# Two halves of P·V that meet in an accumulating transfer, norms of phi in two VectorE operations, and a list scheduler with other durations

## The chip, the cores and the metric

One Trainium2 chip, one of its cores. The metric is the device time of one launch in microseconds (us), the median of several runs. The engines are TensorE (PE; its weight loads are listed apart as PEld), VectorE (DVE), ScalarE (ACT), GpSimd (POOL) and SyncE (SP, which here only issues transfers).

## The reference

```python
# attention with a compressive memory; B, H, S, D = 4, 8, 576, 64
scores = where(causal, -1e9, q @ k.T / sqrt(D));  a = softmax(scores);  local = a @ v
q_p     = phi(q)                                  # phi(x) = x + 1 where x > 0, else exp(x)
mem_out = (q_p @ M_prev) / (q_p @ z_prev + 1e-6)
g       = sigmoid(beta)                           # one number for each head
x = g * mem_out + (1 - g) * local                 # -> 2304 tokens x 512
# two feed-forward layers, d_model 512, d_ff 2048
h = x @ w_in1;  x = (s * relu(h)**2 + b) @ w_out1
h = x @ w_in2;  out = (h * tanh(softplus(h))) @ w_out2
```

## The kernel before

The program has three stages that overlap. **Attention** runs as units, one for each batch b and head h. M_prev stands in front of v as 64 more keys, so that a unit is 5 row tiles of 128 queries (64 of them padding), in two groups: TA (tiles 0 to 2) and TB (tiles 3 and 4). **The first layer** (L801 and L874 on PE) works in blocks of tokens: blocks 0 to 4 of 256, then two big ones of 512; each block is 16 steps, one for each 128 columns of d_ff. **The second layer** (L1006 and L1072) follows.

Most matmuls are in float32r with each operand split into a high and a low part, so that a product costs two or three matmuls. Units of batch 0 are *early* ones: they use plain float32 with one matmul for each product and run in half units, all eight TA halves first, then the TB halves. The other 24 are *full* units. While the early units run, the first layer's weights are loaded and converted from float64, a piece at a time (32 pieces; DVE lines L705 to L718).

In a unit POOL takes min(q, 0) (L498), ACT its exp, DVE makes phi (L500). `norm_phi` (L492) multiplies phi by z and sums over 64 columns, one operation for each row tile; L496 and L504 make the reciprocal, and POOL writes the scaled phi in front of the scores in `Pt` (L555). On the other side scores (PE L534 early, L538 and L539 full) are masked and reduced on DVE (L543), exponentiated on ACT (L552), their sums inverted on DVE (L572, L574), and each tile is scaled by its row's factor (L569) on the engine that a letter string names: `E_NORM = 'PPPDA'` for early units, `F_NORM = 'PPDDA'` for full ones (P is POOL, D DVE, A ACT). PE transposes the tiles (L596) and multiplies by v (L624).

In a full unit that last product has v's high part in output rows 0 to 63 and its low part in rows 64 to 127 of one PSUM bank. ACT copies rows 64 to 127 to `xs` (L632), DVE adds rows 0 to 63 to it (L635), SP stores 64 rows to `x_d` in DRAM (L638). `load_x` reads a block of x back, four transfers into `xr` (`yr` for big blocks), once all its heads have stored (L818); ACT and DVE split it (L819, L820).

The order of work is made ahead of time by a list scheduler, `Plan`: every step has an engine, a duration, a priority and the steps that it waits for, and the next step of an engine is the ready one of the best priority. On the chip each engine works through its list in order and waits by semaphores, so that a POOL step that waits holds all POOL steps behind it. Between 7 and 85 us of the plan's clock PE is given products of zeros (L1242) where it would stand idle.

Of the kernel before, what the change touches and what calls it, by code (L numbers as in the profile page):

```python
# [37 lines left out]
E_TRA, E_NORM, E_XS = 'AAAADA', 'PPPDA', 'A'  # L38
# [19 lines left out]
def pool_us(n):  # L58
    return 0.2 + 0.0033 * n
# [272 lines left out]
def attention_then_two_ffn(ctx: ExitStack, tc: tile.TileContext, qk, qz, vm, beta,  # L332
# [99 lines left out]
    def unit(b, h, prio, groups=(TA, TB), place=None):  # L432
# [94 lines left out]
        def score(t):  # L527
# [31 lines left out]
        def norm(tiles):  # L559
# [15 lines left out]
            for t in tiles:  # L575
                e = on((E_NORM if early else F_NORM)[t])
                n = D + P * t
                us = act_us(n) if e == ACT else 0.05 + dve_us(n, True) if e == DVE else pool_us(n)
# [711 lines left out]
```

## Time and profile before

| | |
|---|---|
| median of 3 runs (lowest, highest) | 1025.32 us (1023.12, 1026.48) |
| the profiled execution | 1026.47 us, of which its span is 1024.7 |
| busy over the span | PE 98%, PEld 91%, DVE 82%, ACT 70%, POOL 20% |
| first layer's block 0 starts, its big blocks start | 81.5 us, 481.8 us |
| second layer's first matmul | 652.2 us |

A PE row's busy time counts overlapping matmuls once, and one of 256 columns is shown as 0.28 us though they follow each other every 0.12 us; so short gaps between matmuls don't show in it. Weight loads (PEld) are shorter and show them better.

### The profile page before, as it was taken

How to read it: one execution, taken by the hardware profiler on the slowest of the kernel's cores; microseconds unless marked ns; L12 is line 12 of the kernel's file. 1: busy time of each engine (PE TensorE's matmuls, PEld its weight loads, DVE VectorE, ACT ScalarE, POOL GpSimd, SP SyncE). 2: the span in 40 equal slices, each digit the busy share in tenths (PEclk: the TensorE clock that was granted, in tenths of full speed). 3: DMA queues.
4: the chain of work that ended last, by engine and by line, in shares of the span. 5: the costliest groups of instructions: out<-in, count | busy, mean ns of one | idle time of the engine just before them, and what ended most of it. 6: DMA issues, size and time to landing. Idle time of an engine off the chain costs nothing.

```text
span 1024.7 us, 20147 instructions
## 1 busy us (share of the span) xinstructions
PE 1000.5 (98%) x6738; PEld 927.6 (91%) x6738; DVE 840.1 (82%) x2403; ACT 713.2 (70%) x1606; POOL 203.9 (20%) x330
## 2 busy tenths in 40 slices
PE   6999998999999999999999999999999999999998
PEld 5567798999999999999888788899999999999998
DVE  6799999999999999996779976269975789667864
ACT  6788897888887788876878987456653466434552
POOL 6752123334333333320000000000000000100000
PEclk9899999999999999999999999999999999999999
DMA  9664662333422333315989885568686666766464
GB/s 259 181 188 142 174 187 91 108 98 105 130 88 90 91 103 92 102 49 179 271 274 305 299 275 170 211 213 269 220 299 222 217 219 205 255 224 221 145 221 170
DMA packets 88984, 188.63 MB, mean 184 GB/s; under 512 B 8752, under 2 KB 63024, under 8 KB 81584
## 3 DMA queue, kind: packets, MB, share of 16 engines
q1 hardware_dynamic: 81392, 135.95, 42.4%
q0 software_dynamic: 7056, 51.38, 14.8%
q8 instruction: 53, 0.87, 0.3%
q14 instruction: 51, 0.42, 0.1%
q10 hardware_dynamic: 432, 0.01, 0.0%
HBM read 144.32 MB, written 42.99 MB: 183 GB/s over the span
## 4 chain that ended last, share of the span: by engine, by line
PE 70%; DVE 9%; issue 7%; DMA 6%; ACT 5%; POOL 2%; SPq 0%; POOLq 0%; DVEq 0%; ACTq 0%
PE bank L1006 15%; PE bank L1072 14%; PE bank L874 13%; PE bank L801 13%; PE bank L624 5%; PE bank L596 4%; PE bank L534 2%; DMA wi_d<-sc 2%; PE bank L538 1%; PE bank L539 1%; POOL Pt L569 1%; DMA stage<-in_w_in 1%; DMA woh<-wo_split_d 1%; PE bank L1242 1%; DMA x_d<-xs 1%
## 5 line engine op out<-in xcount | busy, mean ns | idle before, releaser
L1072 PE MATMUL bank<-woh,S 128*128 128x256 f32 x792 | 107.4, 283 | 1.4 <-DMA woh<-wo_split_d 1.4
L1072 PEld LDWEIGHTS bank<-woh,S 128*128 128x128 f32 x792 | 100.8, 192 | 1.6 <-ACT S L729 1.6
L1072 PE MATMUL bank<-wol,S 128*128 128x256 f32 x720 | 98.1, 283 | 0.0
L555 POOL TENSOR_SCALAR Pt<-ex,nm 128x64 f32<-128x64 f32 x148 | 73.3, 513 | 105.6 <-DVE nm L504 56.3
L1006 PE MATMUL bank<-wi,woh 128*128 128x384 f32 x426 | 93.9, 334 | 0.0
L552 ACT ACTIVATE Pt<-Pt,mx 128x64 f32<-128x64 f32 (+4 forms) x148 | 81.3, 551 | 18.0 <-DVE mx L543 17.7
L1072 PEld LDWEIGHTS bank<-wol,S 128*128 128x128 f32 x720 | 91.8, 192 | 0.0
L987 POOL DMA_DIRECT2D wol<-wo_split_d x17 | 9.2, 541 | 354.1 <-DVE wi L730 262.3
L1006 PEld LDWEIGHTS bank<-wi,woh 128*128 128x128 f32 x426 | 75.6, 188 | 0.6
L1006 PE MATMUL bank<-wi,wol 128*128 128x384 f32 x294 | 75.9, 334 | 0.0
L596 PE MATMUL bank<-ident,Pt 128*128 128x128 f32 x432 | 65.1, 277 | 8.0 <-POOL Pt L569 6.3
L569 POOL TENSOR_SCALAR Pt<-Pt,rs 128x64 f32<-128x64 f32 (+2 forms) x68 | 52.4, 806 | 77.1 <-DVE rs L574 44.6
L543 DVE CUSTOM_DVE_ANT_0 Pt<-bank,mask 128x320 f32<-128x320 f32 (+3 forms) x148 | 59.5, 419 | 9.5 <-PE bank L534 5.2
L604 DVE TENSOR_TENSOR PTl<-bank,PTh 128x128 fp32r<-128x128 f32 (+1 forms) x144 | 64.5, 481 | 1.3 <-ACT PTh L601 0.8
L596 PEld LDWEIGHTS bank<-ident,Pt 128*128 128x128 f32 x432 | 48.7, 141 | 14.2 <-POOL Pt L569 10.5
L601 ACT CAST PTh<-bank 128x128 fp32r<-128x128 f32 (+1 forms) x144 | 54.4, 430 | 4.2 <-PE bank L596 2.4
L1006 PEld LDWEIGHTS bank<-wi,wol 128*128 128x128 f32 x294 | 53.1, 188 | 0.3
L874 PE MATMUL bank<-gl,woh 128*128 128x256 f32 x320 | 53.2, 289 | 0.0
L874 PE MATMUL bank<-gh,wol 128*128 128x256 f32 x320 | 53.2, 288 | 0.0
L874 PE MATMUL bank<-gh,woh 128*128 128x256 f32 x320 | 52.3, 286 | 0.0
L801 PE MATMUL bank<-xh,wi 128*128 128x256 f32 x320 | 50.1, 287 | 0.3 <-DVE rt L852 0.2
L624 PE MATMUL bank<-PTh,V 128*128 128x384 f32 (+1 forms) x192 | 48.1, 277 | 0.0
(277 smaller groups left out, 2894.4 us busy)
## 6 DMA issues: line engine op xcount, KB each, us to landing
wol<-wo_split_d POOLq DMA_DIRECT2D x17, 1024.0 KB, 5.2
woh<-wo_split_d POOLq DMA_DIRECT2D x16, 1024.0 KB, 5.5
qk<-in_qk SPq DMA_DIRECT2D x24, 608.0 KB, 3.9
stage<-in_w_out SPq DMA_DIRECT2D x23, 512.0 KB, 4.9
wo_split_d<-high SPq DMA_DIRECT2D x44, 256.0 KB, 4.3
stage<-in_w_in SPq DMA_DIRECT2D x21, 512.0 KB, 5.2
stage<-wi_d SPq DMA_DIRECT2D x24, 384.0 KB, 5.4
wi_split_d<-woh SPq DMA_DIRECT2D x8, 1024.0 KB, 4.9
```

Source lines behind the costliest of these rows:

```text
L543: nc.vector.tensor_tensor_reduce(Pt[t].t[:, D + lo:D + hi], ps.t[:, :hi - lo], mask[:, SP - w + lo:SP - w + hi], -SCALE, mx.t[:, t:t + 1] ...
L552: nc.scalar.activation(Pt[t].t[:, D:w + D], Pt[t].t[:, D:w + D], AF.Exp, bias=mx.t[:, t + i:t + i + 1], scale=-1.0, accum_out=rs.t[:, t:t ...
L555: add(POOL, 0.3, lambda: nc.gpsimd.tensor_scalar(Pt[t].t[:, :D], ex.t[:, t, :], nm.t[:, t:t + 1], 1.0, op0=ALU.mult, op1=ALU.mult), [ex, n ...
L569: (nc.vector if e == DVE else nc.gpsimd).tensor_scalar(x, x, r, None, op0=ALU.mult)
L596: nc.tensor.transpose(ps.t[:, c - c0, :], Pt[t].t[:, c * P:(c + 1) * P], ident)
L601: (nc.vector.tensor_copy if dve else nc.scalar.copy)(PT[0].t[:, at_], ps.t[:, :n])
L604: nc.vector.tensor_tensor(PT[1].t[:, at_], ps.t[:, :n], PT[0].t[:, at_].bitcast(F32), op=ALU.subtract)
L624: nc.tensor.matmul(o.rearrange("p (t q) -> p t q", q=P), v, x.t[:, f[0]:f[-1] + 1:f[1] - f[0] if len(f) > 1 else 1, :], start=(c == 0 and ...
L801: nc.tensor.matmul(ph, w_at(nm, r, cc)[:, o:o + P], x_at(x, cc), start=(part == 0 and cc == 0), stop=(part == 2 and cc == NCC - 1))
L874: nc.tensor.matmul(acc[ec // per].t[:, (ec % per) * n:(ec % per + 1) * n], w_at(nm, r, jj)[:, ec * P:(ec + 1) * P], t(x), start=(big and f ...
L1006: nc.tensor.matmul(ps.t[:, :H2], w[i // 4].t[:, j, kk, i % 4], x[kk].t[:, k], start=begin and part == kk == 0, stop=part == 2 and kk == 1, ...
L1072: nc.tensor.matmul(acc[t].t[:, :DH], s.t[:, j, t * P:(t + 1) * P], x.t[:, k, q % 4], start=q == part == 0, stop=q == NQ2 - 1 and part == 2)
```

## The change

There are three edits. First, in full units ACT copies all 128 rows of the product to `xs`, the DVE addition goes, and SP stores both halves, to two tensors `x_d[0]` and `x_d[1]`. `load_x` reads `x_d[0]` as before and then POOL issues a second transfer that adds `x_d[1]` to the same tile; it waits for the first to land. It is there for the columns of full units only: 4 of 192 columns in block 2, 4 of 256 in each of blocks 3 and 4, 4 of 512 in each big block; 20 in all, and none for blocks 0 and 1. Second, `norm_phi` becomes one product over all the tiles of a unit and one reduction. Third, the scheduler gets other durations, hops and landing times, and the third letter of `E_NORM` goes from POOL to DVE.

```diff
-E_TRA, E_NORM, E_XS = 'AAAADA', 'PPPDA', 'A'
+E_TRA, E_NORM = 'AAAADA', 'PPDDA'
+ACCUM_LAG = 4.5
 def pool_us(n):
-    return 0.2 + 0.0033 * n
+    return 0.38 + 0.0028 * n
...
         def norm_phi():
-            for t in tiles:
-                nc.vector.tensor_tensor_reduce(qn()[:, t + 1, :], ex.t[:, t, :], qn()[:, 0, :], 1.0, 0.0,
-                                               ALU.mult, ALU.add, nm.t[:, t:t + 1])
+            nc.vector.tensor_tensor(q_rows(), ex.t[:, mine], qn()[:, 0:1, :].to_broadcast([P, n_t, D]), op=ALU.mult)
+            nc.vector.tensor_reduce(nm.t[:, mine], q_rows(), axis=AXIS, op=ALU.add)
...
-            add(POOL, 0.3, lambda: nc.gpsimd.tensor_scalar(Pt[t].t[:, :D], ex.t[:, t, :], nm.t[:, t:t + 1], 1.0,
+            add(POOL, 0.48, lambda: nc.gpsimd.tensor_scalar(Pt[t].t[:, :D], ex.t[:, t, :], nm.t[:, t:t + 1], 1.0,
...
-            if not early:
-                add(DVE, dve_us(m), lambda: nc.vector.tensor_tensor(xs.t[:, :m], pv.t[:D, skip:n], xs.t[:, :m], op=ALU.add),
-                    [pv, xs], [xs])
+            rows = slice(0, D) if early else slice(0, P)
+            add(ACT, act_us(m) - 0.04, lambda: nc.scalar.copy(xs.t[rows, :m], pv.t[rows, skip:n]), [pv], [xs])
-            add(DMA, 0.5, lambda: nc.sync.dma_start(x_d[p0:p0 + D, h // 2, c0:c0 + m], xs.t[:, :m]), [xs], [x_in[b, groups_all.index(g)]])
+            for i in range(1 if early else 2):
+                add(DMA, 0.3, lambda i=i: nc.sync.dma_start(x_d[i][p0:p0 + D, h // 2, c0:c0 + m], xs.t[i * D:(i + 1) * D, :m]),
+                    [xs], [x_in[b, groups_all.index(g)]])
...
+            if n > skip:
+                add(POOL, 1.0, prio, lambda c=c, xr=xr: nc.gpsimd.dma_start(xr.t[:, skip:], x_d[1][:, c, t0 + skip:t0 + n], accum_op=ALU.add,
+                                                                            max_dma_last_dim=1024), [*need, xr], [xr]).lag = ACCUM_LAG
```

The changed program has 2104 DVE rows where there were 2382, 347 POOL rows for 335, 112 stores of x for 64, and 113 products of zeros for 144; the other matmuls are the same in number. Its line numbers are up to 3 higher (L569 becomes L572, L555 L558, L498 L501, L635 goes). Three places show how the order moves.

POOL in the first stage, from the first early TA half on (`Pt_0_158` and its like are the half's three tiles, `B_0_235` a third tile held elsewhere); before:

```order
L569 TENSOR_SCALAR Pt_0_158<-Pt_0_158,rs_160 128x64
L569 TENSOR_SCALAR Pt_0_162<-Pt_0_162,rs_160 128x192
L569 TENSOR_SCALAR Pt_0_174<-Pt_0_174,rs_160 128x320
L555 TENSOR_SCALAR Pt_1_226<-ex_182,nm_212 128x64
L555 TENSOR_SCALAR Pt_1_231<-ex_182,nm_212 128x64
L555 TENSOR_SCALAR B_0_235<-ex_182,nm_212 128x64
L498 TENSOR_SCALAR ex_278<-qn_153 128x192
```

and of the change:

```order
L572 TENSOR_SCALAR Pt_0_168<-Pt_0_168,rs_170 128x64
L572 TENSOR_SCALAR Pt_0_172<-Pt_0_172,rs_170 128x192
L558 TENSOR_SCALAR Pt_1_208<-ex_178,nm_199 128x64
L558 TENSOR_SCALAR Pt_1_214<-ex_178,nm_199 128x64
L558 TENSOR_SCALAR B_0_222<-ex_178,nm_199 128x64
L501 TENSOR_SCALAR ex_260<-qn_148 128x192
```

The half's widest scaling (320 columns) has left POOL; it now stands on DVE. This is so for all eight TA halves.

DVE in a full unit of batch 1, from the last two of its five row sums; before:

```order
L492 ISA qn_2533,nm_2692<-ex_2588,qn_2533 128x64
L492 ISA nm_2692 128x1
L492 ISA qn_2533,nm_2692<-ex_2588,qn_2533 128x64
L492 ISA nm_2692 128x1
L635 TENSOR_TENSOR xs_2707<-bank_112,xs_2707 64x256
L572 TENSOR_SCALAR rs_2650<-rs_2650,igate 128x3
```

and of the change, the like place of another such unit:

```order
L495 TENSOR_TENSOR qn_2974<-ex_3021,qn_2974 128x320
L496 TENSOR_REDUCE nm_3143<-qn_2974 128x5
L499 TENSOR_SCALAR nm_3143<-nm_3143,igate 128x5
L575 TENSOR_SCALAR rs_3091<-rs_3091,igate 128x3
```

Five pairs have become two instructions, and the addition to `xs` is gone.

POOL where block 2 of the first layer is loaded, in both programs from row 157, min(q, 0) of the tenth full unit, on; before:

```order
L498 TENSOR_SCALAR ex_3357<-qn_3297 128x320
L555 TENSOR_SCALAR Pt_0_3455<-ex_3145,nm_3276 128x64
L555 TENSOR_SCALAR Pt_0_3484<-ex_3145,nm_3276 128x64
L555 TENSOR_SCALAR Pt_0_3488<-ex_3145,nm_3276 128x64
```

and of the change:

```order
L501 TENSOR_SCALAR ex_3398<-qn_3346 128x320
L820 DMA xr_3376<-x_d 128x192
L820 DMA xr_3386<-x_d 128x192
L820 DMA xr_3391<-x_d 128x192
L820 DMA xr_3403<-x_d 128x192
L558 TENSOR_SCALAR Pt_1_3450<-ex_3206,nm_3318 128x64
L558 TENSOR_SCALAR Pt_1_3483<-ex_3206,nm_3318 128x64
```

Four accumulating transfers stand ahead of the next unit's L558, each behind a wait for its tile's first load.

Counted in the two orders, before and in the change: ahead of block 0's first L801 PE has 133 and 113 attention matmuls; ahead of its first L820 DVE has 32 and 29 row minima and 15 and 13 converted pieces. Between the TA product of the eighth full unit, the last that block 2 needs, and block 2's first matmul PE has 65 and 132 matmuls. Between attention's last matmul and the first big block's PE has 132 and 180. From the first big block on the markers of the order agree.

## Rows read from the trace of the kernel before

**Rows 1.** Stretches: length, PE, PEld, DVE, ACT, POOL busy, clock, DMA.

```profile
0.00:81.50 81.50, 69.31 (x343) 48.47 (x343) 65.24 (x254) 62.20 (x166) 51.35 (x76) 0.94 0.71 205
81.50:158.40 76.90, 76.32 (x527) 65.27 (x527) 72.97 (x232) 68.68 (x156) 17.98 (x24) 1.00 0.55 165
158.40:481.80 323.40, 317.93 (x2539) 308.41 (x2538) 296.61 (x1120) 259.00 (x684) 108.50 (x182) 1.00 0.34 101
481.80:675.00 193.20, 192.18 (x883) 161.20 (x882) 139.81 (x282) 145.86 (x271) 0.00 (x0) 1.00 0.77 249
675.00:1024.70 349.70, 344.79 (x2453) 344.24 (x2451) 265.47 (x519) 177.50 (x331) 26.08 (x49) 1.00 0.67 225
...
30.00:40.00 10.00, 8.00 (x27) 5.34 (x26) 6.36 (x24) 5.78 (x17) 6.00 (x10) 0.66 0.62 167
```

**Rows 2.** Chain that ended last, 0 to 82 us: start, length, what.

```profile
22.18 1.44 POOL B L569
...
25.84 1.08 POOL Pt L569
26.92 3.70 POOL Pt L555 x2
...
58.73 1.54 POOL Pt L569
```

**Rows 3.** POOL's groups, 0 to 81.5 us: count, busy us, mean ns, idle before.

```profile
L569 POOL TENSOR_SCALAR Pt<-Pt,rs 128x320 f32<-128x320 f32 x4 | 5.6, 1398 | 0.0
L569 POOL TENSOR_SCALAR B<-B,rs 128x320 f32<-128x320 f32 x4 | 4.8, 1212 | 0.0
```

**Rows 4.** DVE's groups over the whole span, the same columns.

```profile
L569 DVE TENSOR_SCALAR Pt<-Pt,rs 128x320 f32<-128x320 f32 x24 | 9.9, 412 | 0.0
L635 DVE TENSOR_TENSOR xs<-bank,xs 64x320 f32<-64x320 f32 x24 | 11.5, 478 | 2.6 <-ACT xs L632 2.4
L635 DVE TENSOR_TENSOR xs<-bank,xs 64x256 f32<-64x256 f32 x24 | 9.9, 414 | 3.8 <-ACT xs L632 3.5
```

**Rows 5.** DVE's timeline in a full unit, 212.7 to 214.2 us: start, length, instruction.

```profile
212.41 0.49 DVE L500 SCALAR_TENSOR_TENSOR ex<-qn,ex 128x320 f32<-128x320 f32 x1
212.82 0.48 DVE L635 TENSOR_TENSOR xs<-bank,xs 64x320 f32<-64x320 f32 x1
213.22 0.22 DVE L492 CUSTOM_DVE_ANT_0 qn<-ex,qn 128x64 f32<-128x64 f32 x1
213.37 0.07 DVE L492 DVE_READ_ACCUMULATOR2_ANT nm<- 128x1 f32 x1
...
214.02 0.47 DVE L857 SCALAR_TENSOR_TENSOR gl<-rt,sb,gh 128x256 fp32r<-128x256 f32 x1
```

**Rows 6.** Weight loads, 81.5 to 481.8 us; last, PEld's idle time by releaser.

```profile
L596 PEld LDWEIGHTS bank<-ident,Pt 128*128 128x128 f32 x387 | 43.4, 140 | 6.6 <-POOL Pt L569 3.8 <-issue 1.1 <-DVE Pt L569 0.6
L801 PEld LDWEIGHTS bank<-xh,wi 128*128 128x128 f32 x320 | 42.8, 190 | 1.7 <-DVE rt L852 0.9 <-issue 0.5
L624 PEld LDWEIGHTS bank<-PTl,V 128*128 128x128 f32 x192 | 36.5, 190 | 2.0 <-DVE PTl L604 2.0
L539 PEld LDWEIGHTS bank<-B,A 128*128 128x128 f32 x144 | 27.4, 190 | 2.1 <-DVE B L513 1.8
L538 PEld LDWEIGHTS bank<-B,A 128*128 128x128 f32 x144 | 27.3, 190 | 3.2 <-DVE PTl L604 1.5 <-DVE xs L635 0.8 <-DVE PTl L601 0.2
```

**Rows 7.** Timelines: x of block 2, its first matmuls, big x.

```profile
250.82 0.45 SPq L638 DMA_DIRECT2D x_d<-xs  x1
252.04 3.72 SPq L818 DMA_DIRECT2D xr<-x_d  x4
258.51 1.77 PE L801 MATMUL bank<-xh,wi 128*128 128x256 f32 x10
...
466.96 0.45 SPq L638 DMA_DIRECT2D x_d<-xs  x1
469.01 1.76 SPq L818 DMA_DIRECT2D yr<-x_d  x4
481.80 0.86 PE L801 MATMUL bank<-yh,wi 128*128 128x512 f32 x3
```

**Rows 8.** Issues on POOL (ns); KB and us to landing.

```profile
L987 POOL DMA_DIRECT2D wol<-wo_split_d x17: 527/528/737, 715.8 to 999.9; - x17
wol<-wo_split_d POOLq DMA_DIRECT2D x17, 1024.0 KB, 5.2
xr<-x_d SPq DMA_DIRECT2D x20, 128.0 KB, 3.5
yr<-x_d SPq DMA_DIRECT2D x8, 256.0 KB, 6.4
```

**Rows 9.** L555 on POOL: shortest, median, longest ns; DVE beside the longest (timeline).

```profile
L555 POOL TENSOR_SCALAR Pt<-ex,nm x148: 307/353/3097, 6.8 to 452.9; 128x64 f32<-128x64 f32 x148
26.05 0.86 DVE L709 CUSTOM_DVE_ANT_0 stage<-wil,stage 128x1024 uint16<-128x1024 uint16 x1
28.61 0.69 DVE L718 TENSOR_TENSOR wi<-stage,wi 128x512 fp32r<-128x512 f32 x1
```

More of the change, by code (lines that the diff above doesn't have):

```diff
@@ L375, in attention_then_two_ffn @@
     sb = const.tile([P, 2], F32, name="sb")
-    x_d = dram.tile([P, NCC, NT], F32, name="x_d")
+    x_d = [dram.tile([P, NCC, NT], F32, name=f"x{i}_d") for i in range(2)]
     y_d = dram.tile([P, NCC, NT], F32, name="y_d")
@@ L432, in unit, with add @@
     def unit(b, h, prio, groups=(TA, TB), place=None):
-        def add(engine, us, f, r=(), w=(), keep=(), share=1.0):
+        def add(engine, us, f, r=(), w=(), keep=(), share=1.0, lag=0.0):
             attention_steps.append(plan.add(engine, us, prio, f, r, w, keep=keep, share=share))
+            attention_steps[-1].lag = lag
         early = place is not None and place < 5
         first_half = groups == (TA,)
+        late = 1.3 if early else 0.0
         tiles = [t for g in groups for t in g]
@@ L577, in norm @@
                 n = D + P * t
-                us = act_us(n) if e == ACT else 0.05 + dve_us(n, True) if e == DVE else pool_us(n)
+                us = act_us(n, 1) if e == ACT else 0.08 + dve_us(n, True) if e == DVE else pool_us(n)
                 add(e, us, lambda t=t, e=e: scale(t, e), [done, Pt[t]], [Pt[t]], [rs])
@@ L642, in unit @@
         norm(groups[0])
[L643 removed]
+        add(DMA, 0.6 * nb / NQ, lambda: nc.sync.dma_start(vx(), vm[b, h][:, :nb]), w=[vx_b], lag=late)
         if not early:
@@ L691, in convert @@
         add(DMA, 1.5, prio, lambda: nc.sync.dma_start(words(), src.bitcast(I32).rearrange("p (n two) -> p n two", two=2)),
-            w=[raw], after=after).lag = 1.0 if layer == 1 else 3.0
+            w=[raw], after=after).lag = 1.4 if layer == 1 else 3.0
         e = on((C_W if layer == 1 else C2_W)[j])
-        add(e, 0.52 if e == ACT else 0.335, prio,
+        add(e, 0.567 if e == ACT else 0.335, prio,
             (lambda: nc.scalar.activation(f32(), words()[:, :, 1].bitcast(F32), AF.Copy, scale=2.0 ** -112)) if e == ACT else
@@ L845, in first @@
             add(PE, 0.48 if not big else 0.908, prio, lambda part=part: mm_in(ph.t[:, :n], xh, xl, fc, part), need, [ph])
-        add(ACT, act_us(n) - 0.04, ew, lambda: nc.scalar.activation(
+        add(ACT, act_us(n) - (0.04 if big else -0.06), ew, lambda: nc.scalar.activation(
             rt.t, ph.t[:, :n], *((AF.Relu,) if big else (AF.Copy, 0.0, sb[:, 0:1]))), [ph], [rt])
@@ L853, in first @@
                 [ph, rt], [rt])
-        add(ACT, act_us(n), ew, (lambda: nc.scalar.copy(t(gh), rt.t)) if big else
+        add(ACT, act_us(n) + (0.0 if big else 0.1), ew, (lambda: nc.scalar.copy(t(gh), rt.t)) if big else
             (lambda: nc.scalar.activation(t(gh), rt.t, AF.Identity, sb[:, 1:2])), [rt], gh_bufs + ([gg] if big else []))
-        add(DVE, dve_us(n), ew, (lambda: nc.vector.tensor_tensor(t(gl), rt.t, t(gh).bitcast(F32), op=ALU.subtract)) if big else
+        add(DVE, dve_us(n) + (0.0 if big else 0.06), ew, (lambda: nc.vector.tensor_tensor(t(gl), rt.t, t(gh).bitcast(F32), op=ALU.subtract)) if big else
             (lambda: nc.vector.scalar_tensor_tensor(t(gl), rt.t, sb[:, 1:2], t(gh).bitcast(F32), op0=ALU.add, op1=ALU.subtract)),
```

30 lines of the change are left out of this document (13 added, 17 removed).

## The prediction

> **What bounds the kernel now.** I read the stages first [rows 1]. From 81.5 us on, PE is busy 99%, 98%, 99% and 99% of the stretches, and in the last one the weight loads too (344 of 350 us). From 481.8 us on PE alone sets the time, and the order there is the same in both programs; a gain has to come from before. Before 81.5 us no engine is full: PE 69.3, DVE 65.2, ACT 62.2 and POOL 51.4 of 81.5 us, and PE's figure holds 143 products of zeros. This stage waits in a chain, for block 0 of the first layer can't begin before all eight TA halves are stored. From 81.5 to 481.8 us PE and DVE are both nearly full (DVE 73.0 of 76.9 us, then 296.6 of 323.4), so that each loses a little to the other.
>
> Second, the chain of the first stage [rows 2]: POOL carries much of it, the widest scalings of tiles among them (1.44, 1.08, 1.54 us), and a pair of L555 that took 3.70 us. Third, who ended PEld's idle time in the middle stage [rows 6]: DVE 7.8 us (0.6, 0.9, 2.0, 1.8, and 1.5 + 0.8 + 0.2), POOL's L569 3.8. These 11.6 us are all that other engines visibly take from PE in 400 us.
>
> **The first stage: -4 us.** Eight 320-column scalings leave POOL, 5.6 + 4.8 = 10.4 us [rows 3]. Three of them stand on the chain with 1.44 + 1.08 + 1.54 = 4.06 us [rows 2]. On DVE one takes 0.41 us [rows 4], 3.3 us in all, on an engine that is free 16 us of this stage. Bounds: 10.4 us if every one held a half up, nothing if DVE is as late as POOL was. I take 4, what the chain shows.
>
> The new order also puts less ahead of block 0: 13 converted pieces for 15, 29 row minima for 32. That is about a tenth of DVE's 65.2 us, 6.5, less the 3.3 that it takes over: 3 us. So block 0 starts near 74.5 us. But what was put off is done later, when PE is full: 20 attention matmuls at the next stretch's pace (527 in 76.9 us, 0.146 each) are 2.9 us. Of the 7 us 4 stay. Bounds: +1 (the chain doesn't shorten, the deferred work costs) and -8 (10.4 + 3 - 2.9, less 2.5 for the L555 that then lead).
>
> The norm in two operations costs these halves about what it cost; POOL's better known durations only reorder.
>
> **The middle stage: -4 us.** In 24 full units the additions to `xs` go. A DVE operation here holds the engine some 0.08 us less than its length: the 0.48 us one at 212.82 is followed at 213.22, after 0.40 [rows 5]. So 24 x (0.40 + 0.33) = 17.5 us leave DVE [rows 4].
>
> The norms: five row sums ran from 213.22 to 214.02, 0.80 us, the reads of the accumulator beside the next operation [rows 5]. The new pair are two passes over 320 columns. A product or a copying operation of that width holds DVE 0.40 us (L500 at 212.41, L635 at 212.82), a scaling 0.41 - 0.08 = 0.33 [rows 4, 5]; a reduction isn't in the trace. From 2 x 0.33 to 0.40 + 0.80, if the reduction needs twice the time, a unit wins 0.14 or loses 0.40, over 24 units -3 to +10 us of DVE. I take 0.80, no change, as the reduction reads the same columns once.
>
> [...] In the trace five short sums cost what I give two long operations [rows 5]. [...]
>
> What are 17.5 us of 369.6 us of DVE worth? If DVE alone set the pace, all of it; if PE did, nothing. PE's visible waits for DVE are 7.8 us [rows 6], and the two engines fill up alike. I take half of these waits, 4 us, and put the rest at what PE needs anyway. ACT copies 128 rows instead of 64 with the same columns, no more time. SP has 48 more stores of 0.45 us [rows 7], spread over the 320 us of the full units; the loads queued behind one come 0.45 us later, which the units in flight hide.
>
> **The accumulating transfers: 0.** Block 2 is the place where x is late. Before, its last store is issued at 250.82 and its first matmul starts at 258.51, 7.7 us [rows 7]. The change adds the second store (0.45), four issues on POOL (0.53 each, 2.1) and one more landing. The landing of an accumulating transfer isn't in the trace: 3.5 us for a plain load of 128 KB by SP is the nearest below, 5.2 for 1024 KB issued by POOL the nearest above [rows 8]. The chain then takes 13.8 to 15.5 us. The order has 132 matmuls between the product that feeds that store and block 2, at 2539 in 323.4 us [rows 1] 16.8 us of work; before it had 65, 8.3 us, for a chain of 7.7. So the cover has grown with the chain, by a little over a microsecond to spare. Without it PE would lose up to the landing, 5 us.
>
> Each transfer waits in POOL's queue for its tile's first load, and behind the four stand the next unit's L558; who waits for those is PE's transposes. A hold of 2 us there is inside what POOL has free (108.5 of 323.4 us busy). For the first big block, before, the last store is issued at 466.96, its loads from 469.01, and its first matmul is at 481.80 [rows 7]; the loads take 6.4 us [rows 8], so x and its split are there by about 478. With the transfers it is some 8 us later, while the order now has 180 matmuls there for 132, 5.8 us more cover besides the 4 that were free. Blocks 3 and 4 are loaded far ahead of their use. From the first big block on nothing changes.
>
> **The sum.** The profiled execution took 1026.47 us, its span 1024.7 and 1.8 around it. 1026.5 - 4 - 4 + 0 = 1018.5. It stands 1.2 above the median of the runs shown, so a median of the changed kernel should be near 1017.
>
> **Rivals.**
>
> *POOL's queue becomes the wait (slower).* An operation on POOL can be stretched by DVE: L555 takes 0.31 us at its shortest and 3.10 at its longest, and beside the longest DVE ran L709 and L718, which read two inputs from SBUF [rows 9]. If DVE does that to the accumulating issues, four take 12.4 us instead of 2.1: block 2's x is 10.3 us later, 9 beyond the cover, and at half speed without the first layer PE loses 4.5 there; the L558 behind are held as long at blocks 2, 3 and 4, about 4 us of PE each time beyond what two units in flight hide. That is 16 us, 1033. It decides from issues of about 1.5 us on. Against it: POOL's plain issues took 0.527 to 0.737 us [rows 8], beside a DVE busy for 265 of 350 us [rows 1]. [...] Chance 0.14.
>
> *The gain is taken back (no change).* If the first stage waits for DVE's conversions rather than POOL, only 3 us come, 2.9 are paid later, and if in the middle PE is bound by its own stream, the freed DVE time is idle: 1025. For it speaks that PE's busy figure is 98% there. Chance 0.20.
>
> *DVE is the real bound of the middle stage.* Then the 17.5 us come off whole, with 4 in the first stage: 1026.5 - 21.5 - 1.2 = 1004. DVE's 95% between 81.5 and 158.4 us speaks for it; but there it converts weights, which doesn't change, and later it is at 92%. Chance 0.17.
>
> [...]
>
> **How the numbers follow.** My forecast, 1017, has 0.45, with 1010 to 1022.2 as its own range. DVE as the bound has 0.17, around 1004; no change 0.20, between 1022 and 1028; POOL's queue 0.14, from 1028 up to 1040; 0.04 is for what I don't see. 0.3% of 1025.3 is 3.1 us, about what a measurement of this kernel can tell from no change. Faster: 0.45 + 0.17 + 0.04 of the third = 0.66; within 0.3%: 0.17; slower: 0.17. The range from 1005 to 1029 leaves out half of the DVE case and most of the slow one, about 0.2.
>
> **What the profile will show.** Block 0's first matmul near 74.5 us (81.5 now), the first big block's near 473.8 (481.8), and the same 543 us from there to the end. POOL's 320-column scalings gone and the first stage's POOL at about 41 us; DVE in the middle stage near 352 us for 369.6; the two operations of the norm near 0.80 us together; the accumulating issues at 0.53 us, their landings at 3.5 to 5.2; PE's wait for block 2 under 1 us. Wrong, if the landings take over 6.5 us (block 2 starves), if block 0 doesn't come earlier, or if PE's idle time for DVE vanishes and matmul counts rise to those of the last stage (then DVE was the bound).

## The result and the profile after

The changed kernel took 1031.97 us in the median of four runs (1030.65 to 1033.81), the kernel before 1025.69 beside it: a ratio of 1.0067, with an interval from 1.0043 to 1.0091. It is 0.67% slower, where 1017 us was forecast. Its profiled execution took 1030.65 us, 4.2 more than that of before.

The stretches of the changed kernel, cut at the same times as [rows 1], columns as there:

```profile
0.00:81.50 81.50, 71.01 (x371) 50.37 (x372) 70.86 (x232) 66.36 (x177) 43.81 (x68) 1.00 0.72 208
81.50:158.40 76.90, 74.20 (x505) 62.50 (x503) 72.28 (x203) 65.42 (x148) 15.60 (x24) 1.00 0.49 157
158.40:481.80 323.40, 311.55 (x2492) 307.18 (x2493) 283.38 (x894) 254.72 (x685) 126.59 (x201) 0.98 0.45 122
481.80:675.00 193.20, 191.70 (x878) 159.67 (x877) 135.25 (x278) 142.35 (x266) 1.20 (x1) 1.00 0.79 252
675.00:1028.70 353.70, 348.18 (x2468) 347.04 (x2466) 266.23 (x519) 178.95 (x333) 26.09 (x49) 1.00 0.66 222
```

DVE lost 13.2 us in the third stretch and POOL 7.5 in the first, as the change meant. But PE has 47 matmuls fewer in the third stretch and its clock a mean of 0.98: something there keeps it waiting. The first matmul of the first layer came at 68.1 us (81.5 before), yet the first big block's at 483.0 (481.8).

To find where a lead goes, I count PE's work by the widths of the matmuls that have begun (0.06 us for 128 columns up to 0.227 for 512, more for the plain float32 ones of the early halves, where 256 columns follow each other every 0.216 us and full units' every 0.120; products of zeros left out). It is 936 us in every kernel here. The table, computed from the traces, gives the time at which the kernel before has done so much, and how much later (+) or earlier (-) the others have. It is one execution of each, which can stand a few us from its median: e9 is the same program as the changed kernel up to 249 us, and yet stands 4.8 us from it at work 117. What a kernel loses from one column to the next varies less: from 80 to 117 the changed kernel, e3, e9 and e10, all the same program up to there, lose 10.1 to 10.9 us.

```
work done          20     80    110    117    190    240    385    400    480    560    930
before           55.9  130.9  163.7  175.0  253.2  308.5  464.2  479.4  559.6  641.1 1015.1
after            -6.7   -9.3   -6.0   +0.8   +0.1   -2.2   -6.5   +1.2   +1.7   +2.8   +4.0
e1 accum alone   -3.1   -3.9   -2.1   +2.7   +1.7   +3.7   +4.2   +9.6  +11.8  +15.7  +16.2
e2 no accum      -5.8   -9.2   -2.5   -1.7   -2.0   +0.4   -0.3   -0.4   -0.4   -2.1   -1.9
e3 loads behind  -5.5   -7.8   -4.6   +2.8   +2.0   +0.6   -1.7   -1.8   -1.8   -1.6   -1.6
e5 norm on POOL  -0.2   -3.2   -1.6   +0.3   +0.4   +8.2   +5.4   +6.3   +6.5   +9.8  +10.5
e6 low on POOL   -4.1   -5.7   -0.8   +5.4   +4.1   +3.5   +5.0   +5.5   +5.5   +5.8   +6.2
e7 units later   -6.8   -9.2   -5.9   +0.4   -1.3   -0.5   -3.9   -3.7   -3.7   -3.8   -3.2
e8 e2 + e6       -6.3   -9.0   -4.4   -3.0   -4.1   -5.0   -7.1   -7.2   -7.2   -8.9   -8.7
e9 plain second  -2.5   -5.3   -2.1   +5.6   +5.8   +3.8   +0.7   +4.5   +4.5   +3.5   +4.9
e10 no transfer  -6.2   -9.0   -5.6   +1.4   +0.8   -2.1   -5.6   -5.7   -5.7   -7.4   -9.0
e13 low twice    -4.0   -5.9   +0.3   +9.3   +8.6   +7.7   +5.0   +7.5  +12.6  +15.2  +15.8
e14 low to POOL  -6.2   -8.9   -5.2   +1.8   +1.2   -0.8   -4.1   +0.6   +3.0   +4.8   +3.5
e17 less DVE     -6.8   -9.2   -5.7   +0.8   +0.1   -1.5   -5.3   -1.2   -0.6   +0.9   -0.5
e18 durations    -2.4   -5.8   +0.6   +0.2   +0.4   +2.6   +1.2   +1.1   +1.1   -0.5   +0.3
```

So the change gains twice and loses twice: 9.3 us ahead at 131 us, all lost by 176 (6.8 of it after 158); 6.6 us gained between 253 and 458; 7.7 lost at once at the first big block; 2.8 more after it.

**The first loss.** Windows of 5 us of the changed kernel, same columns:

```profile
150.00:155.00 5.00, 4.96 (x42) 4.76 (x41) 5.00 (x14) 4.99 (x12) 0.00 (x0) 1.00 0.28 82
155.00:160.00 5.00, 3.56 (x28) 3.14 (x26) 4.91 (x11) 3.65 (x8) 1.99 (x2) 1.00 0.33 85
160.00:165.00 5.00, 1.97 (x11) 1.51 (x11) 4.93 (x20) 3.59 (x11) 2.41 (x5) 1.00 0.58 204
165.00:170.00 5.00, 2.69 (x11) 1.96 (x11) 4.92 (x14) 4.25 (x10) 2.06 (x3) 0.64 0.13 39
170.00:175.00 5.00, 4.93 (x30) 4.93 (x31) 4.30 (x11) 2.50 (x6) 3.25 (x6) 0.68 0.39 113
```

DVE is full while PE stands, and after PE's idling the clock is granted at 0.64 and 0.68 in the last two windows. The waits from 150 to 172 us (engine, line, releaser: total, times, longest):

```profile
POOL Pt L558 <- DVE nm L507: 8.9, 2, 8.4
PEld bank L599 <- POOL Pt L572: 3.6, 2, 3.0
PE bank L599 <- POOL Pt L572: 3.2, 2, 2.8
PEld bank L542 <- DVE B L516: 1.8, 1, 1.8
PEld bank L627 <- DVE PTl L607: 1.8, 1, 1.8
```

These belong to the first full units, which go through ACT, DVE and POOL in turn while the last weights are still converted.

**The second loss.** Windows of the changed kernel at the first big block:

```profile
460.00:465.00 5.00, 5.00 (x44) 5.00 (x44) 1.82 (x4) 1.46 (x3) 3.72 (x3) 1.00 0.82 240
465.00:470.00 5.00, 4.59 (x39) 4.39 (x37) 0.00 (x0) 0.00 (x0) 1.21 (x1) 1.00 1.04 257
470.00:475.00 5.00, 0.45 (x2) 0.45 (x3) 1.92 (x4) 2.49 (x5) 0.00 (x0) 0.86 0.96 160
475.00:480.00 5.00, 5.00 (x25) 5.00 (x25) 4.65 (x11) 4.87 (x10) 2.39 (x3) 0.50 0.67 180
```

SP's queue there, and under it POOL's (timelines: start, length, instruction):

```profile
456.88 2.74 SPq L818 DMA_DIRECT2D yr<-x_d  x4
459.67 0.91 SPq L691 DMA_DIRECT2D stage<-in_w_in  x2
460.62 0.43 SPq L691 DMA_DIRECT2D raw<-in_w_in  x1
```

```profile
460.43 3.72 POOL L820 DMA_DIRECT2D yr<-x_d  x3 [15.20 <-DMA yr<-x_d]
465.49 1.21 POOL L820 DMA_DIRECT2D yr<-x_d  x1 [1.33 <-DMA yr<-x_d]
```

The waits from 465 to 482 us, and the DMA issues from 455 to 477 us (KB each, median us to landing):

```profile
ACT yh L822 <- DMA yr<-x_d: 8.7, 2, 8.5
PEld bank L801 <- DVE rt L855: 5.2, 1, 5.2
```

```profile
yr<-x_d POOLq DMA_DIRECT2D x4, 256.0 KB, 12.1
raw<-in_w_in SPq DMA_DIRECT2D x1, 512.0 KB, 11.1
```

The first halves are issued from 456.9 us; behind them SP at once issues three loads of second-layer weights, 1.5 MB; the accumulating transfers are issued from 460.4 us, beside and behind these, and land 10.9 to 13.0 us after issue, all after the three loads. ACT stands in order at the split of x (8.5 us), so the products that the first layer still has to do get no new input (PE's wait for L855), PE is busy 0.45 of 5 us, and then it runs 5 us with the clock granted at 0.50. Before, the first big block's x came whole with the four loads issued from 469.01 us [rows 7], ahead of the weight loads.

### The profile page after: what moved, and what is told of

The parts are those of the page before. It is cut to its first block, busy times and chain, and to the rows that moved or that the text cites. A ratio compares the mean times of both kernels' runs of the same rounds, so it can differ in the third digit from the quotient of the medians.

```text
span 1028.7 us, 19852 instructions
## 1 busy us (share of the span) xinstructions
PE 996.6 (97%) x6707; PEld 926.8 (90%) x6707; DVE 828.0 (80%) x2123; ACT 707.8 (69%) x1606; POOL 213.3 (21%) x342
## 4 chain that ended last, share of the span: by engine, by line
PE 68%; issue 17%; DMA 6%; DVE 5%; POOL 2%; ACT 2%; SPq 0%; POOLq 0%; ACTq 0%; DVEq 0%
PE bank L877 18%; PE bank L801 18%; PE bank L1009 9%; PE bank L1075 6%; PE bank L627 6%; PE bank L599 5%; PE bank L542 2%; PE bank L537 2%; PE bank L541 1%; DMA yr<-x_d 1%; DMA xr<-x_d 1%; DMA woh<-wo_split_d 1%; DMA woh<-wi_split_d 1%; DMA x_d<-xs 1%; DVE Pt L546 1%
## 5 line engine op out<-in xcount | busy, mean ns | idle before, releaser
L558 POOL TENSOR_SCALAR Pt<-ex,nm 128x64 f32<-128x64 f32 x148 | 75.7, 571 | 121.7 <-PE bank L599 80.2
L555 ACT ACTIVATE Pt<-Pt,mx 128x64 f32<-128x64 f32 (+4 forms) x148 | 81.6, 553 | 9.7 <-DVE mx L546 8.9
L1009 PEld LDWEIGHTS bank<-wi,woh 128*128 128x128 f32 x450 | 79.5, 188 | 0.9 <-DMA woh<-wi_split_d 0.3
L1009 PE MATMUL bank<-wi,wol 128*128 128x384 f32 x270 | 69.5, 335 | 0.1
L546 DVE CUSTOM_DVE_ANT_0 Pt<-bank,mask 128x320 f32<-128x320 f32 (+3 forms) x148 | 60.3, 419 | 4.0 <-PE bank L537 2.1
L572 POOL TENSOR_SCALAR Pt<-Pt,rs 128x64 f32<-128x64 f32 x64 | 48.5, 830 | 53.8 <-DVE rs L577 31.3
L801 PE MATMUL bank<-xh,wi 128*128 128x256 f32 x320 | 50.8, 287 | 0.1
L1009 PEld LDWEIGHTS bank<-wi,wol 128*128 128x128 f32 x270 | 48.7, 188 | 0.6 <-DMA wol<-wi_split_d 0.3
```

The costliest lines, as they stand in the source:

```text
L546: nc.vector.tensor_tensor_reduce(Pt[t].t[:, D + lo:D + hi], ps.t[:, :hi - lo], mask[:, SP - w + lo:SP - w + hi], -SCALE, mx.t[:, t:t + 1] ...
L555: nc.scalar.activation(Pt[t].t[:, D:w + D], Pt[t].t[:, D:w + D], AF.Exp, bias=mx.t[:, t + i:t + i + 1], scale=-1.0, accum_out=rs.t[:, t:t ...
L558: add(POOL, 0.48, lambda: nc.gpsimd.tensor_scalar(Pt[t].t[:, :D], ex.t[:, t, :], nm.t[:, t:t + 1], 1.0, op0=ALU.mult, op1=ALU.mult), [ex, ...
L572: (nc.vector if e == DVE else nc.gpsimd).tensor_scalar(x, x, r, None, op0=ALU.mult)
L801: nc.tensor.matmul(ph, w_at(nm, r, cc)[:, o:o + P], x_at(x, cc), start=(part == 0 and cc == 0), stop=(part == 2 and cc == NCC - 1))
L1009: nc.tensor.matmul(ps.t[:, :H2], w[i // 4].t[:, j, kk, i % 4], x[kk].t[:, k], start=begin and part == kk == 0, stop=part == 2 and kk == 1, ...
```

## The experiments

Each ran in five rounds beside the kernel before (1024.5 to 1026.1 us there). The ratios:

| run | median us | ratio to before, interval |
|---|---|---|
| e1 accum alone | 1042.59 | 1.0162, 1.0131 to 1.0193 |
| e2 no accum | 1024.45 | 0.9983, 0.9970 to 0.9996 |
| e3 loads behind | 1025.17 | 0.9994, 0.9977 to 1.0011 |
| e4 five sums | 1035.34 | 1.0078, 1.0054 to 1.0102 |
| e5 norm on POOL | 1034.51 | 1.0098, 1.0076 to 1.0120 |
| e6 low on POOL | 1032.71 | 1.0083, 1.0064 to 1.0101 |
| e7 units later | 1024.76 | 1.0004, 0.9991 to 1.0017 |
| e8 e2 and e6 | 1018.13 | 0.9940, 0.9922 to 0.9958 |
| e9 plain second | 1026.98 | 1.0019, 0.9999 to 1.0039 |
| e10 no transfer | 1021.28 | 0.9956, 0.9939 to 0.9974 |
| e11 2 KB pieces | 1032.59 | 1.0077, 1.0048 to 1.0106 |
| e12 before, low on POOL | 1025.78 | 0.9995, 0.9980 to 1.0010 |
| e13 low twice | 1036.11 | 1.0104, 1.0077 to 1.0131 |
| e14 low to POOL, same order | 1035.02 | 1.0079, 1.0054 to 1.0105 |
| e15 scalings to DVE | 1037.38 | 1.0104, 1.0082 to 1.0126 |
| e16 accum in batch 1 | 1025.16 | 0.9995, 0.9982 to 1.0008 |
| e17 less DVE | 1030.16 | 1.0051, 1.0035 to 1.0067 |
| e18 durations alone | 1025.10 | 0.9996, 0.9984 to 1.0008 |

### The parts of the change

**e1**, the kernel before with the diff's parts on `xs`, `x_d` and `load_x` alone.

> The kernel before with the accumulating transfers alone (both halves stored, the second added on loading); norms, durations and the order's numbers stay those of before. My theory (the gain is real, and is taken back at the first big block, whose four accumulating transfers queue behind 1.5 MB of second-layer weight loads): the last PV product ends 4 to 10 us before 465.8 us, the first big block's four transfers land 9 to 13 us after their issue and it starts no earlier than 478 us; time 1021 to 1028 us. Rival one (accumulating transfers are slow whatever is beside them): also the blocks of 256 columns wait, the starts of blocks 2 to 4 move later by 3 us or more against before; time over 1030 us. Rival two (the loss comes from the new durations, not from the transfers): the first big block starts by 474 us, time 1012 to 1019 us.

The landings (10.4 to 11.1 us) and the big block's late start (491.4) came as the theory had them. The time did not, nor did the last product of P and v, which ends 1.7 us earlier than before and not 4 to 10. Rival one's signs came too: blocks 2 to 4 begin 7 to 12 us later. The old order has less cover: it loses 5.4 us at the first big block and 3.9 at the second. Rival two is out.

**e2**, the changed kernel with these parts undone.

> The changed kernel without the accumulating transfers: the two halves are added on DVE as before, with the new norms, durations and order numbers. My theory: the gap at 468 to 475 us and the half-clock stretch behind it go, DVE's 17.5 us of additions come back; the first big block starts at 470 to 477 us, the stall at 150 to 175 us stays; time 1019 to 1026 us, under the changed kernel by 5 us or more. Rival two (new durations and order lose by themselves): the stall at 150 to 175 us is as large and the time is 1029 us or more.

As the theory had it, 8.6 us under the changed kernel in ratio; no loss at the big block. Only the block's start, 481.4 us, is not at 470 to 477. PE still loses 7.5 us of lead by 175 us, so that loss isn't the transfers'. The dense stretch gains nothing here (-2.0 to -0.3), where the changed kernel gained 6.6.

**e4** and **e18**, the five sums of the norms put back into the orders of the changed kernel and of e2.

```diff
-            nc.vector.tensor_tensor(q_rows(), ex.t[:, mine], ..., op=ALU.mult)
-            nc.vector.tensor_reduce(nm.t[:, mine], q_rows(), axis=AXIS, op=ALU.add)
+            for t in tiles:
+                nc.vector.tensor_tensor_reduce(...)
```

> The changed kernel with the norms of phi as before (five multiply-and-sum operations of 64 columns in place of a product and a sum over 320), in the same order of instructions on every engine. My theory (the two forms cost the same, 0.80 us a unit): within 0.3% of the changed kernel, 1029 to 1035 us. Rival three (the two-operation form is the loss): 1024 us or less; if it is instead a gain on DVE, 1036 us or more.

> The kernel of e2 with the norms as before the change (five sums), in e2's order: the kernel before with the new durations and the moved scaling alone. If the two forms of the norms cost the same (my prediction), within 0.2% of e2, 1022 to 1027 us. If the new form saves DVE time (e4 against the changed kernel points to 1 us or so), 1025 to 1029 us.

The sums cost 0.11% and 0.13% against the pair, within the intervals. The durations and the moved scaling by themselves change nothing (0.9996).

### The first big block

**e3**, the weight loads behind the transfers.

```diff
-        add(DMA, 1.5, prio, lambda: nc.sync.dma_start(words(), ...), w=[raw], after=after)
+        behind = layer == 2 and len(raw_steps) < 3 * 6
+        queue = nc.gpsimd if behind else nc.sync
+        add(POOL if behind else DMA, ..., -2.0 if behind else prio, lambda: queue.dma_start(words(), ...),
+            w=[raw], after=[*after, *accumulated] if behind else after)
```

> The changed kernel with one thing moved: the first three second-layer weight loads (512 KB each) are issued on POOL's queue behind the first big block's four accumulating transfers, not on SP's ahead of them. My theory (queueing behind these loads): the four transfers land 4 to 7 us after issue in place of 10.9 to 13.0 us, the first big block starts at 472 to 477 us in place of 483, no half clock behind it; time 1021 to 1026 us. Rival one (accumulating 256 KB is slow by itself, 3 to 4 us each, one after another): they still land 9 to 13 us after issue, time 1029 to 1033 us.

The four landed after 4.8, 5.3, 6.5 and 7.1 us. The first big block started at 480.1, since this execution's earlier stages were later too, and no work was lost there (-1.7 to -1.8 in the table). Up to 474 us PE, DVE and ACT work in the changed kernel's order, so that nothing else stands between the two. The windows of e3:

```profile
465.00:470.00 5.00, 5.00 (x44) 5.00 (x43) 1.69 (x4) 1.68 (x4) 4.90 (x4) 1.00 0.90 198
470.00:475.00 5.00, 5.00 (x44) 5.00 (x43) 2.90 (x5) 2.60 (x6) 1.68 (x3) 1.00 1.12 197
475.00:480.00 5.00, 5.00 (x43) 4.97 (x42) 2.73 (x6) 2.88 (x7) 0.29 (x1) 1.00 0.96 319
```

PE stays full (5.00 of 5 us) and its clock at 1.00. Where the three loads stand is worth 0.73%, 7.5 us, as much as the change had lost.

**e9**, the second transfers as plain loads.

```diff
-  nc.gpsimd.dma_start(xr.t[:, skip:], x_d[1][...], accum_op=ALU.add, max_dma_last_dim=1024)
+  nc.gpsimd.dma_start(xr.t[:, skip:], x_d[1][...], max_dma_last_dim=1024)
```

> The changed kernel with its second transfers of x as plain loads, not accumulating ones: the same bytes, queue, waits and order on every engine, but the second half overwrites the first and is not added, so the output is not the reference's. It separates what accumulating costs from what one more transfer behind the first costs. If the price is the queueing behind the weight loads (my theory of the first big block), the four transfers of the first big block still land 9 to 12 us after issue and the time is 1029 to 1033 us. Rival (adding on the way into SBUF makes the transfers slow): they land within 4 to 7 us, those of block 2 within 4 us in place of 3.0 to 7.7, and the time is 1022 to 1027 us.

Both have a part. The first big block's transfers landed after 8.7 to 9.7 us, as the theory had it, so most of the delay is the queue. Adding makes them longer: 10.9 to 13.0 us in the changed kernel, 9.1 to 11.9 in the six other runs of its order (e4, e11, e13 to e15 and e17). In blocks 2 to 4 it is 2.4 to 5.5 us plain and 3.0 to 7.8 accumulating, the third and fourth of a group the slow ones. The time, 1026.98 us, is in the rival's range: leaving out the adding alone gives back 0.48%, 4.9 us. How much of that is at the big block, one execution doesn't settle: the loss there is 3.8 us for 7.7, but e14 and e17, which add, lose 4.8 and 4.1.

**e11**, `max_dma_last_dim=2048` for 1024.

> The changed kernel with rows of 2 KB in the big blocks' accumulating transfers in place of two pieces of 1 KB (the size argument 2048 for 1024); all else the same. If the pieces' number sets the landing (rival), the big blocks' transfers land 3 us or more sooner and the time is 1025 to 1029 us; if it is the queueing behind the weight loads (my theory), they land within 1 us of before and the time stays at 1030 to 1034 us.

No change, as the theory had it: landings of 10.5 to 11.7 us, a ratio of 1.0077.

**e10**, the second transfers left out (`if n > skip` made false).

> The changed kernel without the second transfers of x at all: both halves are stored, the second is never read, so the output is not the reference's; the order is planned anew. It gives what freeing DVE of the additions, the new norms and the new durations bring when nothing has to be paid for them. My prediction's steps (4 us in the first stage, 4 us in the middle, nothing lost afterwards): 1014 to 1020 us. Rival (DVE's bound at 125 to 175 us eats it all; the additions off DVE are worth nothing): within 2 us of e2, 1022 to 1026 us.

0.9956, between the two ranges and 0.27% under e2 (the intervals just overlap): freed of its price, taking the additions off DVE is worth some 3 us, and the change as a whole 4.5. Its profiled execution, 3.7 us under its median, shows the same loss at 158 to 176 us and a gain of 6.4 in the dense stretch.

**e16**, accumulating for batch 1 alone.

```diff
+LAST_ACCUM = 1
...
+            added = b > LAST_ACCUM
...
+        top = min(n, (LAST_ACCUM + 1) * S - t0)
...
-            if n > skip:
+            if top > skip:
```

> The changed kernel with the accumulating transfers for the second batch's x alone (8 units, blocks 2 to 4); the 16 units of the last two batches add their halves on DVE and store one x, so the big blocks have no second transfer; planned anew. If accumulating pays where no weight loads are queued ahead: a third of e10's dense-stage gain over e2 stays (2 us), 1019 to 1023 us. Rival (it costs in blocks 2 to 4 what it frees): as e2 or slower, 1024 to 1030 us.

The rival held: 0.9995, no better than e2.

### The stretch up to 176 us

**e7**, `UNIT0` 92.65 for 84.65, on e3.

> The kernel of e3 with the priorities of the full attention units and of the first layer's blocks 8 us later (one number of the plan), nothing else changed. My theory (DVE is the bound at 125 to 175 us, whatever comes first): the place of the stall moves, but the starts of blocks 2 and 3 stay within 2 us of e3's 261.8 and 341.2 and the time within 3 us of e3. Rival (the full units were started too early, on top of the weight conversions): the stall falls to about the 8 us of the kernel before, time 1016 to 1021 us.

The time is e3's, as the theory had it (block 3 came 3.3 us sooner), and the loss between 131 and 175 us is 9.6 us for e3's 10.6. But this is no test of the stall: the new priorities leave the orders of PE, ACT and DVE as they are in e3 up to 163 us. Neither later nor earlier units were tried there.

**e5**, e3 with `E_NORM` 'PPPDA'.

> The kernel of e3 (weight loads behind the transfers), with the scaling of the third attention tile in the early units back on POOL, as before the change (eight operations of 320 columns, 0.40 us each on DVE), and the order planned anew. My theory (between 125 and 175 us DVE is the bound, so that a unit's work moved onto DVE earlier is paid there): 3.2 us less on DVE, the stall at 125 to 175 us (17 us of PE's time in e3, 8 in the kernel before) shrinks by 2 to 4 us, though block 0 starts later than in e3, and the time is 1020 to 1024 us. Rival (the order of the units makes the stall): stall unchanged within 1.5 us, time 1024 to 1030 us.

Half right, and the time wrong. The loss between 131 and 175 us is 3.5 us for e3's 10.6, but the lead was only 3.2. Then, in this order, block 2's transfers were issued from 254.4 and the last landed at 264.7 too late for PE:

```profile
260.00:265.00 5.00, 2.98 (x14) 2.72 (x15) 2.42 (x8) 2.19 (x9) 0.46 (x1) 0.80 0.87 249
265.00:270.00 5.00, 3.88 (x16) 2.86 (x15) 4.36 (x14) 2.14 (x6) 3.23 (x5) 0.52 0.56 151
```

That is 7.8 us of PE, with the stretches in which the clock was granted at 0.80 and 0.52.

**e6** (on e3), **e8** (on e2) and **e12** (on the kernel before), eight of the low-part subtractions on POOL.

```diff
-            hi_dve, lo_dve = C_HI[j] == "D", C_LO[j] == "D"
+            hi_dve, lo_dve = C_HI[j] == "D", r < 2 or j % 2 == 0
```

> The kernel of e3 with eight of the sixteen low-part subtractions of the last two quarters of the first layer's weights (0.6 us each on DVE) on POOL, the order planned anew. My theory (DVE is the bound at 125 to 175 us): 4.8 us less on DVE there, the stall shrinks by 3 to 5 us, time 1019 to 1022 us. [...]

> The kernel of e2 (halves added on DVE) with the same eight low-part subtractions on POOL as in e6. My theory: as in e6 3 to 5 us under the kernel without them, 1019 to 1022 us, within 0.3% of e6, since the additions taken off DVE in e6 buy little once the weights are converted. If removing the additions is worth what the middle stage of e3 showed against e2 (5 us of PE's waits between 175 and 450 us), e6 ends 4 us or more under this one.

> The kernel before with nothing but the eight low-part subtractions of the first layer's last weights on POOL, as in e8. If DVE is the bound at 125 to 175 us whatever the order's numbers, this alone gives 3 to 5 us: 1020 to 1023 us. If e8's gain needs the new durations and norms too, it is within 2 us of the kernel before, 1023 to 1028 us.

Against the kernel that each edits, the same edit gave +0.9%, -0.4% and nothing, so "4.8 us off DVE" doesn't predict the time. e6 is slower than its range, e8 a little faster than its own. e8, without the transfers, is the best kernel of the study: 0.9940, faster than both, and 14.6 us under e6, which differs from it by the transfers, the moved weight loads and the order.

**e13** and **e14**, the last quarter's subtractions doubled on DVE, or given to POOL, without a new order.

```diff
-                lambda: (nc.vector if lo_dve else nc.gpsimd).tensor_tensor(w_at(lo, r, j), ...),
+                lambda: [nc.vector.tensor_tensor(w_at(lo, r, j), ...) for _ in range(1 + (r == 3))],   # e13
+                lambda: (nc.gpsimd if r == 3 else nc.vector).tensor_tensor(w_at(lo, r, j), ...),      # e14
```

> The changed kernel with the low-part subtractions of the last quarter of the first layer's weights issued twice on DVE (same result; 8 times 0.69 us more on DVE up to 171 us), every other engine's order unchanged. If DVE is the bound up to 175 us (my theory), PE comes 4 to 6 us later out of that stretch and the time rises by 3 to 6 us, to 1035 to 1038 us. Rival (DVE has slack there, the wait is another's): under 1.5 us later, time 1031 to 1034 us.

> The changed kernel with the same eight subtractions issued on POOL in place of DVE, planned as before, so that PE, ACT and SP keep their order. If DVE is the bound up to 175 us (my theory), PE comes 3 to 5 us earlier out of that stretch and the time falls to 1026 to 1029 us. Rival: no earlier, 1031 us or more; if POOL's own queue is the wait (1.3 us each ahead of its scalings), later by up to 5 us.

At work 117 e13 is 8.5 us later than the changed kernel, but 3.4 of these stood at 80 already, ahead of the added work, and this execution took 6.4 us more than its median. From 80 to 117 it loses 15.2 us for 10.1, about the 5.5 added; the medians differ by 0.37%, 3.8 us, as the theory had it. Taking off brought nothing (+1.8 in e14 for +0.8, and 1035.02 us). In e14 single operations of DVE on SBUF took longer beside POOL's subtractions, five of them 0.35 to 1.1 us longer than in the changed kernel, 3.9 us together; those that read PSUM banks did not (means of L855 0.416 us in both, of L546 with 320 columns 0.484 for 0.487). DVE's groups in the changed kernel (140 to 175 us), then DVE and POOL in e14 (timelines):

```profile
L709 DVE CUSTOM_DVE_ANT_0 stage<-stage 128x1024 uint16<-128x1024 uint16 x5 | 3.4, 679 | 0.0
L707 DVE TENSOR_SCALAR stage<-stage 128x512 uint16<-128x512 uint16 x4 | 3.0, 750 | 0.0
```

```profile
159.67 1.64 DVE L709 CUSTOM_DVE_ANT_0 stage<-stage 128x1024 uint16<-128x1024 uint16 x1
163.07 0.49 DVE L546 CUSTOM_DVE_ANT_0 Pt<-bank,mask 128x320 f32<-128x320 f32 x1
```

```profile
159.28 1.49 POOL L718 TENSOR_TENSOR wol<-stage,woh 128x512 fp32r<-128x512 f32 x1 [6.46 <-ACT woh L715]
162.05 1.52 POOL L718 TENSOR_TENSOR wol<-stage,woh 128x512 fp32r<-128x512 f32 x1
```

**e15**, the two small scalings of each full unit on DVE, same order (`nc.vector if e == DVE or not early`).

> The changed kernel with POOL's scalings of the first two attention tiles in the 24 full units (0.55 and 0.93 us each there) issued on DVE in place of POOL, planned as before, so that PE, ACT and SP keep their order; some 0.3 us more on DVE per unit, 7 us in all. Rival (PE waits for POOL's scalings at 160 to 166 us, 3.5 us of its waits): 3 us or more of the stretch come back, time 1026 to 1030 us. My theory (DVE full): the waits move to DVE's, time 1030 to 1036 us.

PE's wait for `Pt` became one for DVE (2.2 us for the 3.2 on POOL), as the theory had it; the time is above both ranges. POOL's slow scalings aren't the cause.

**e17**, the AND left out for the last quarter (`None if layer == 1 and r == 3 else ...`).

> The changed kernel with one of the four DVE operations of each conversion left out for the last quarter of the first layer's weights (the AND with 0x8000, 0.75 us each, eight times 0.75 = 6.0 us), nothing put in its place and no other engine's order changed; these weights then are not the right ones, so the output is not the reference's. If DVE is the bound up to 175 us (my theory), PE comes 5 to 9 us earlier out of that stretch than in the changed kernel (4 to 8 us ahead of the kernel before at the same work), and the time falls by 3 to 7 us, to 1025 to 1029 us. Rival (another wait stands there): under 2 us earlier, time 1030 us or more.

PE came out of the stretch exactly as late (+0.8). So the 6 us of work taken off DVE, seven eighths of it before 157 us, are not what holds it, though adding to DVE (e13) does harm. Where PE stands, DVE is still busy 4.93 of 5 us; its work in that place was not changed. Windows of e17:

```profile
155.00:160.00 5.00, 3.63 (x30) 3.37 (x28) 4.23 (x10) 3.95 (x9) 2.87 (x5) 1.00 0.42 114
160.00:165.00 5.00, 1.97 (x11) 1.51 (x11) 4.93 (x20) 3.75 (x12) 0.99 (x2) 1.00 0.54 183
165.00:170.00 5.00, 2.89 (x12) 1.97 (x13) 4.55 (x13) 4.29 (x11) 2.37 (x3) 0.69 0.13 39
```

What remains is the order. ACT's rows of the changed kernel, then of the kernel before, where the second full unit's first operation on ACT stands (`A<-qk`):

```profile
154.71 0.69 ACT L698 ACTIVATE stage<-stage 128x512 f32<-128x512 f32 x1
155.28 0.68 ACT L703 ACTIVATE stage<-stage 128x512 int32<-128x512 uint32 x1
155.84 0.73 ACT L512 CAST A<-qk 128x640 fp32r<-128x640 f32 x1
```

```profile
148.15 0.77 ACT L567 ACTIVATE Pt<-Pt,rs 128x576 f32<-128x576 f32 x1
148.82 0.72 ACT L509 CAST A<-qk 128x640 fp32r<-128x640 f32 x1
```

It stands 7.0 us later, right behind two of a conversion's operations (L698, L703), though its input had landed at 142.1 us. In nine kernels it stands at 154.6 to 161.4 us (the changed one, e3, e7, e10, e13 to e17), and PE loses 6 to 9 us between work 110 and 117; but PE and ACT work in one and the same order there in all nine, so they count as one case. In e2, e5, e8 and e18 it stands at 138.5 to 143.4, and PE loses at most 2 there; but e2, e8 and e18 lose 4.6 to 6.7 between 80 and 110 instead, and e6 (146.6) in both places. No kernel kept the lead that it had at 131 us; e8 kept most, 3 of 9 us. No run moved this unit alone, so the order as the cause is argued, not shown, and what holds the lead back in every order stays open.

## Why the prediction was wrong

- **"The accumulating transfers: 0 ... From the first big block on nothing changes."** This step failed, and it is the difference between no change and slower. I gave the first big block's x 8 us more, from landings of 3.5 and 5.2 us that were measured elsewhere [rows 8]; the last one landed 11.2 us after the last plain load (476.4 and 465.2 us), 10.9 to 13.0 after its issue. I counted matmuls as cover and not the bytes that SP issues in between. The price could be read before: the 6.4 us of [rows 8] is the median of two groups that I took for one. The first big block's four loads stood ahead of the weight loads, the second's behind them. Here are SP's queue and then the landings of the two groups, in the kernel before:

```profile
470.81 0.91 SPq L691 DMA_DIRECT2D stage<-in_w_in  x2
471.75 0.43 SPq L691 DMA_DIRECT2D raw<-in_w_in  x1
473.59 3.20 SPq L818 DMA_DIRECT2D yr<-x_d  x4
```

```profile
L818 SPq DMA_DIRECT2D yr<-x_d x4: 332/426/428, 469.0 to 470.3; - x4
DMA to landing us min/median/max: 2.6/3.5/4.0
```

```profile
L818 SPq DMA_DIRECT2D yr<-x_d x4: 320/384/552, 473.6 to 476.5; - x4
DMA to landing us min/median/max: 8.8/9.3/9.7
```

  Plain second transfers behind the weight loads took as long (e9, 8.7 to 9.7). e3 shows what the place costs, 7.5 us. After the first big block 2.8 us more were lost, where I had put nothing.
- **The first stage, -4 us.** Block 0 came at 68.1 us, 13.4 earlier and 6 more than forecast, POOL's busy time there fell to 43.8 (41 forecast). But a lead isn't a gain until nothing behind it waits for somebody else: I subtracted 2.9 us for work put off and let the rest stand, and by 176 us all was gone. e18, the durations and the scaling alone, is worth 0 us. The rival "gain taken back" had this right; its reason, DVE's conversions, is not confirmed by e14 and e17. What took the lead stays open.
- **The middle stage, -4 us.** Right in kind: from 253 to 458 us PE gained 6.6 us in the changed kernel, 3.6 to 5.4 in the runs of its order in the table (e9, e13, e14, e17), and e10 against e2, 0.27%, says some 3 in the medians. That it is all due to the additions is not shown: e8, which still adds on DVE, gained 3.0 there. DVE as the real bound, 17.5 us whole, was wrong.
- **The norms, 0.** Right within the measurement (e4, e18: 0.11 and 0.13%, about 1 us in favour of the pair). In the profile's timeline the pair holds DVE 0.93 us, 0.13 more than the five sums [rows 5]:

```profile
210.63 0.49 DVE L495 TENSOR_TENSOR qn<-ex,qn 128x320 f32<-128x320 f32 x1
211.16 0.49 DVE L496 TENSOR_REDUCE nm<-qn 128x5 f32<-128x320 f32 x1
211.56 1.47 DVE L607 TENSOR_TENSOR PTl<-bank,PTh 128x512 fp32r<-128x512 f32 x3
```

- **Block 2's cover.** It held in the changed kernel, though the landings took up to 7.7 us for 5.2, past the 6.5 named as the sign of failure. It didn't hold in e5 (7.8 us). The margin of "a little over a microsecond" depended on the order.
- **POOL's queue as the wait.** The issues follow one another every 0.55 to 0.75 us (0.53 forecast) and show as 0.89 to 2.03 us each; nobody was held by them. The slow side came from the queue of the transfers and from the adding, not from POOL's queue.

So by the medians the 0.67% divide into -4.5 us for the change without its transfers (e10), +7.5 for their place behind the weight loads (e3), and the rest, +3.9, for the transfers themselves, each known to within 2 or 3 us. It is one way to divide: with the place kept and only the adding left out (e9) 4.9 us come back, so the two prices are not independent.

## What to carry to other kernels

Price a transfer on a critical path by what all queues have issued shortly before it (here 1.5 MB, which took 8.2 to 11.1 us to land), not by its own size, and put the loads that nobody waits for behind it. A median over transfers in two places can hide the slow half; ask for each place by itself. A lead at one stage counts only as far as the next point at which the order waits for another engine; compare the time at which equal work is done, not the start of one block. Work taken off a full engine needs the order planned anew around it, or it may bring nothing.

## What the runs showed of the hardware

An accumulating transfer of 96 to 128 KB landed after 3.0 to 7.8 us, a plain one in its place after 2.4 to 5.5 (e9). Four of 256 KB, issued with 1.5 MB of loads ahead, all landed after the loads, 10.9 to 13.0 us after issue (9.1 to 11.9 in six other runs of the same order); plain ones behind the same loads took 8.7 to 9.7 from POOL (e9) and 8.8 to 9.7 from SP (before). Beside POOL's subtractions of two inputs (1.49 and 1.52 us) single operations of DVE on SBUF took longer: L709 1.64 us in e14 where it takes 0.68 in the changed kernel, so that a part of what left DVE came back (3.9 us of 5.5). PE, busy 0.45 of the 5 us from 470 us, had its clock granted at 0.50 in the next 5 us, about 2.5 us of work lost by an estimate from these rows. ACT's copy of 128 rows by 320 columns took 0.42 us, as that of 64 rows did before (L634 and L632).
